# Three edits in one: where weight pieces are converted, turns moved from TensorE to VectorE, and tile addresses, in a sigmoid-attention and gated-MLP kernel

## Chip, cores and metric

One NeuronCore of a Trainium2 chip. The metric is the device time of one launch in microseconds (us), the median of three runs. TensorE (PE) multiplies; VectorE (DVE), ScalarE (ACT) and GpSimd (POOL) do the elementwise work; SyncE (SP) issues nearly all DMAs, in program order.

## The reference, cut to what matters

```python
# B, H, S, D = 4, 12, 448, 64;  d_model 768, d_ff 1024; w_in and w_out are float64
scores = q @ k.T / sqrt(D) - log(S);  attn = 1 / (1 + exp(-scores));  x = heads joined(attn @ v)
for layer in (1, 2):                  # first: relu; second: tanh-gelu, gain g_ln, residual
    h = act(x @ w_in);  u, v = h[..., :512], h[..., 512:]
    v_n = (v - mean) / sqrt(var + 1e-6) * g
    v_s = einsum('ts,bsd->btd', w_spatial, v_n) + b_spatial[None, :, None]
    x = (x if layer == 2 else 0) + (u * v_s) @ w_out
```

## The kernel before, in words

Every product is taken as three float32r products of a high and a low part (hi·hi, hi·lo, lo·hi): a value is cast to float32r (`hi`), and `lo` is the value less `hi`.

**Order.** Attention runs first, in twelve groups of four heads. Then come eight rounds, named here layer.batch: 1.0, 1.1, 1.2, 1.3, 2.0, 2.1, 2.2, 2.3. The order of instructions is written out by hand and each engine takes its own in that order. A round's TensorE steps are `hv` (the v half of w_in: four steps of 18 matmuls of 512 columns in an even round, three in an odd one, whose fourth key block went with the round before), `hu` (the u half, four steps of 18 matmuls of 448 columns), `sp` (the spatial product, four of 11) and `wo` (four of 18, in six PSUM banks). They run as hv1..hv3 (hv1, hv2 in an odd round), hu0, hu1, hu2, sp0, hu3, sp1, wo0, sp2, wo1, sp3, wo2, then the next round's hv0, then wo3. `hv`, `hu` and `sp` share two PSUM banks. After `sp(i)` VectorE makes `gt` and `u` from PSUM, ScalarE casts `gh`, and VectorE makes `gl`; `wo(i)` needs both. The next round's x is split (`split_x`) into `xh` and `xl` in three steps.

**Belts.** After nearly each TensorE step stands `fill()`, which moves side jobs on by one stage: first `spatial` (the spatial weights), then `belt` (weight pieces), then `chain` (the second half of the norm, and `gl`). A weight piece (`convert`, 128x256) is loaded as float64 words by DMA, rounded to float32 by four VectorE operations (L164, L168, L172, L177) and a ScalarE square (L163), and either split (ScalarE cast L185, VectorE subtract L187) or stored to DRAM (`kept`). `refetch` brings a kept piece back and splits it. Layer 1's w_in (24 pieces) is converted in attention, its w_out (12 pieces) and layer 2's w_in (24) in rounds 1.0 to 1.2; round 1.3, called the refill, refetches layer 2's w_in and converts its w_out (12).

**Turns.** Spatial weights are loaded in four blocks and turned by 16 TensorE transposes a layer into a PSUM bank (L218), then cast and subtracted (L219, L220). The output of a batch of layer 2 is turned in the rounds that follow by `store`: six transposes (L585) into PSUM, a ScalarE copy, and a DMA of rows of 3072 bytes; ten such stores in all. The last batch is turned at the end by `store_last`.

**Addresses.** A tile's byte address inside a partition is the sum of the sizes before it. In the kernel before, these begin 32 bytes behind a multiple of 64: x, bb, vh, vl, uh, ul, sh, sl, the normed v pairs (v0, v1), u, gt, gh, gl. These begin at a multiple of 64: ident, w, f, g, wsp, ops, xh, xl, oh, ol, vr.

Of the kernel before, what the change touches and what calls it, by code (L numbers as in the profile page):

```python
# [25 lines left out]
def tile_sigmoid_attention_two_gated_mlps(  # L26
# [120 lines left out]
    def convert(src, n, part, at, keep, early=False):  # L147
# [3 lines left out]
        w = stg.tile([P, PIECE, 2], I32, tag="w", name="w")  # L151
# [4 lines left out]
        g = stg.tile([P, PIECE], F32, tag="g", name="g", bufs=2)  # L156
# [18 lines left out]
        yield  # L175
# [26 lines left out]
    def load_w_sp(L, j, room, wait=1):  # L202

        w = stg.tile([CP, NCH, P], F32, tag="sp", name="wsp", bufs=2)
        src = L.w_sp.rearrange("(c p) s -> p c s", p=CP)
        if j < 3:
            nc.sync.dma_start(out=w, in_=src[:, :, j * P:(j + 1) * P])
        else:
            for r in range(0, P, REST):
                nc.sync.dma_start(out=w[:, :, r:r + REST], in_=src[:, :, 3 * P:])  # L210
        for _ in range(wait):
            yield
# [3 lines left out]
        t = room()  # L216
        for c in range(NCH):
            nc.tensor.transpose(t[:, c * CP:(c + 1) * CP], w[:, c, :], ident[:CP, :CP])  # L218
        nc.scalar.copy(out=L.sh[:, j, REST:], in_=t[:, :S])  # L219
        nc.vector.tensor_tensor(  # L220
            out=L.sl[:, j, REST:], in0=t[:, :S], in1=raw(L.sh[:, j, REST:]), op=ALU.subtract
        )
        yield
        for w in (L.sh, L.sl):
            nc.vector.tensor_copy(out=w[:, j, :REST], in_=raw(w[:, j, S:]))

    def load_w_sp_pair(L, j):
        yield from load_w_sp(L, j, bank, 7)
        yield
        yield from load_w_sp(L, j + 2, bank, 2)  # L230
# [24 lines left out]
    def load_vecs(L):  # L255
# [12 lines left out]
    kept = dram.tile([P, PIECE * l2.late], F32, name="kept")  # L268
    belt, chain, spatial = Belt(), Belt(), Belt()
    spatial.waiting = [load_w_sp(l1, j, lambda: two_banks()[:, 0]) for j in range(4)]  # L270


    def attention(apool, epool, ps_att, done):
# [52 lines left out]
        def low(n, eng):  # L326
            for j, t, e in zip((1, 3), turned[n], (nc.vector, eng)):
                e.tensor_tensor(
                    out=ops[n][:, j], in0=t, in1=raw(ops[n][:, j - 1]), op=ALU.subtract
                )  # L330
# [64 lines left out]
        load_qk(0)  # L395
        load_v(0)
        load_qk(1)
        turn(0)
        high(0)
        low(0, nc.vector)  # L400
        load_v(1)
        load_vecs(l1)
        for s in range(4 * NG + 2):
# [9 lines left out]
            if n + 1 < NG:  # L413
# [4 lines left out]
                elif r == 2:  # L418
                    low(n + 1, nc.gpsimd)
# [152 lines left out]
    def rows(pr, j):  # L572

        if j == 3:
            return [(slice(r * REST, (r + 1) * REST), out[2 * pr + r, 3 * P:]) for r in range(2)]
        return [(slice(0, P), out[2 * pr + j // 4, j % 4 * P:(j % 4 + 1) * P])]

    def store(pool, pr, j):
        x = xs[pr]
        o = pool.tile([P, DM], F32, tag="o", name="o", bufs=2)  # L580
        t = two_banks()
        half = DM // 2
        for m in range(KD):
            g, c = divmod(m * P, half)
            nc.tensor.transpose(t[:, g, c:c + P], x[:, m, j * P:(j + 1) * P], ident)  # L585
        nc.scalar.copy(out=o.rearrange("p (g f) -> p g f", g=2), in_=t[:, :, :half])
        for ps, dst in rows(pr, j):
            nc.sync.dma_start(out=dst, in_=o[ps])

    def store_last(o, pr, m):  # L590
# [11 lines left out]
        if m % 2:  # L602
# [5 lines left out]
            for ps, dst in rows(pr, 3):  # L608
                eng.dma_start(out=dst[:, ms], in_=o[ps, 0, ms])

    with tc.manual_schedule():
# [23 lines left out]
        with tc.tile_pool(name="fpool", bufs=1) as fpool:  # L635
# [3 lines left out]
            belt.waiting += [convert(*x, kept) for x in l2.pieces[:l2.late]]  # L639
# [111 lines left out]
```

## Time and profile before

| | |
|---|---|
| median of 3 runs | 627.3 us (626.49 to 628.46) |
| the profiled execution's own time | 629.11 us |
| its span, first to last instruction | 626.5 us |
| busy in the span: PE, DVE, ACT, POOL | 596.5, 385.9, 262.1, 95.7 us |
| mean granted TensorE clock | 0.985 |

Matmuls overlap, so PE counts as busy while only waiting for columns; the start-to-start distance of its instructions says more.

### The profile page before, as it was taken

The page shows a single profiled execution, that of the slowest core. Times are in us where ns is not written, and L with a number is a line of the kernel's source. Part 1 is how long each engine was busy: PE and PEld are TensorE (multiplying, and loading weights), DVE is VectorE, ACT ScalarE, POOL GpSimd, SP SyncE. Part 2 cuts the span into 40 slices and gives each one's busy share as a digit, 9 for nine tenths or more (in the row PEclk, how much of TensorE's full clock was granted, in tenths as well). Part 3 has the DMA queues.
Part 4 walks back from the last instruction along what each step waited for, and adds up shares of the span by engine and source line. Part 5 has one row for each costly group of instructions (what it writes and reads, how often), then busy time and mean ns, then how long its engine had stood idle before and what let it go on. Part 6 is the DMA issues. An engine that isn't in the chain of part 4 may idle for free.

```text
span 626.5 us, 9499 instructions
## 1 busy us (share of the span) xinstructions
PE 596.5 (95%) x3660; PEld 471.4 (75%) x3660; DVE 385.9 (62%) x770; ACT 262.1 (42%) x440; POOL 95.7 (15%) x121
## 2 busy tenths in 40 slices
PE   3999999999989899989999997899999999999996
PEld 2555555554779789978998996679889988998995
DVE  5399999996887867776452467772451543244123
ACT  3677777777344333424222453632113313221312
POOL 0164455453120010001000000010010001001000
PEclk9999999999999899989999998899999999999999
DMA  6646446541223224333200253300001000200103
GB/s 191 191 147 187 155 146 187 157 122 35 65 66 85 67 84 143 102 104 98 76 1 1 75 148 107 100 0 1 0 1 76 0 1 18 84 1 0 76 0 101
DMA packets 42044, 50.15 MB, mean 80 GB/s; under 512 B 9872, under 2 KB 30736, under 8 KB 42000
## 3 DMA queue, kind: packets, MB, share of 16 engines
q1 hardware_dynamic: 41840, 49.43, 25.9%
q8 instruction: 28, 0.46, 0.3%
q10 hardware_dynamic: 160, 0.13, 0.1%
q14 instruction: 16, 0.13, 0.1%
HBM read 40.90 MB, written 8.65 MB: 79 GB/s over the span
## 4 chain that ended last, share of the span: by engine, by line
PE 78%; DVE 13%; ACT 4%; DMA 2%; issue 2%; POOL 0%; SPq 0%; ACTq 0%; DVEq 0%; POOLq 0%
PE t L502 17%; PE t L456 13%; PE sc L342 12%; PE av L366 11%; PE sc L555 10%; PE t L521 9%; PE av L555 5%; DVE xl L445 2%; DVE f L168 2%; DVE f L172 1%; DVE f L177 1%; PE sc L585 1%; DVE f L164 1%; DVE st L466 1%; DMA w<-in_moe_w_out_dram 1%
## 5 line engine op out<-in xcount | busy, mean ns | idle before, releaser
L353 ACT ACTIVATE a<-sc,bias_s 128x896 f32<-128x896 f32 (+1 forms) x96 | 92.8, 1007 | 30.6 <-PE sc L342 30.3
L342 PEld LDWEIGHTS sc<-ops 32*128 32x128 f32 x1152 | 56.8, 191 | 46.5 <-ACT a L353 25.9
L342 PE MATMUL sc<-ops 32*128 32x448 f32 x1152 | 79.3, 394 | 10.0 <-ACT ops L324 8.0
L502 PE MATMUL t<-xh,uh 128*128 128x448 f32 x192 | 72.2, 376 | 4.0 <-ACT u L506 3.7
L456 PE MATMUL t<-vh,xh 128*128 128x512 f32 x168 | 68.5, 408 | 5.2 <-DVE sl L220 5.2
L502 PE MATMUL t<-xl,uh 128*128 128x448 f32 x192 | 71.2, 371 | 0.0
L502 PE MATMUL t<-xh,ul 128*128 128x448 f32 x192 | 71.2, 371 | 0.0
L468 POOL TENSOR_SCALAR rs<-mv 128x1 f32<-128x1 f32 x28 | 9.8, 351 | 389.1 <-DVE mv L467 389.1
L456 PE MATMUL t<-vh,xl 128*128 128x512 f32 x168 | 67.6, 402 | 0.0
L456 PE MATMUL t<-vl,xh 128*128 128x512 f32 x168 | 67.5, 402 | 0.0
L521 PE MATMUL t<-sh,v 128*128 128x448 f32 x224 | 65.8, 363 | 0.0
L534 ACT CAST gh<-u 128x448 fp32r<-128x448 f32 x32 | 18.1, 567 | 109.6 <-DVE u L533 109.6
L366 PE MATMUL av<-a,vt 128*64 128x448 f32 x288 | 62.7, 558 | 0.0
L466 DVE BATCH_NORM_STATS2 st<-vr 128x6 f32<-128x512 f32 x28 | 19.4, 694 | 63.6 <-ACT vr L462 63.6
L555 PE MATMUL sc<-gl,oh 128*128 128x448 f32 x128 | 48.8, 381 | 5.4 <-DVE gl L538 5.4
L177 DVE SCALAR_TENSOR_TENSOR f<-g,f 128x256 f32<-128x256 f32 x72 | 50.5, 701 | 1.9 <-ACT u L506 0.5
L529 DVE SCALAR_TENSOR_TENSOR gt<-t,gc,bb 128x448 f32<-128x448 f32 x16 | 10.9, 684 | 63.6 <-PE t L521 63.6
L555 PE MATMUL sc<-gh,oh 128*128 128x448 f32 x128 | 48.5, 379 | 0.0
L555 PE MATMUL sc<-gh,ol 128*128 128x448 f32 x128 | 48.2, 377 | 0.0
L521 PE MATMUL t<-sl,v 128*128 128x448 f32 x128 | 46.7, 365 | 0.0
L521 PEld LDWEIGHTS t<-sh,v 128*128 128x128 f32 x224 | 42.0, 187 | 3.4
L502 PEld LDWEIGHTS t<-xh,uh 128*128 128x128 f32 x192 | 36.5, 190 | 9.0 <-ACT u L506 4.5
(88 smaller groups left out, 1021.5 us busy)
## 6 DMA issues: line engine op xcount, KB each, us to landing
w<-in_moe_w_in_dram SPq DMA_DIRECT2D x48, 256.0 KB, 3.1
w<-in_moe_w_out_dram SPq DMA_DIRECT2D x24, 256.0 KB, 2.7
ink<-in_k_dram SPq DMA_DIRECT2D x12, 448.0 KB, 4.4
inq<-in_q_dram SPq DMA_DIRECT2D x12, 448.0 KB, 5.1
vt<-in_v_dram SPq DMA_DIRECT2D x48, 96.0 KB, 2.6
out_dram<-o SPq DMA_DIRECT2D x9, 384.0 KB, 2.6
kept<-f SPq DMA_DIRECT2D x24, 128.0 KB, 1.7
w<-kept SPq DMA_DIRECT2D x6, 256.0 KB, 3.2
```

The lines of the kernel that those rows point to most:

```text
L168: nc.vector.scalar_tensor_tensor(out=f.bitcast(U32), in0=low.bitcast(U32), scalar=29, in1=f.bitcast(U32), op0=ALU.logical_shift_right, op1 ...
L177: nc.vector.scalar_tensor_tensor(out=f, in0=g, scalar=TINY * TINY, in1=f, op0=ALU.is_ge, op1=ALU.mult)
L342: nc.tensor.matmul(sc[h // 2][:, h % 2, :S], w[ps, o:o + P], ops[n][ps, y, S * j:S * (j + 1)], start=(t == 0), stop=(t == 5), tile_positio ...
L353: nc.scalar.activation(a[:, 2 * x:2 * x + 2] if r < 3 else a[ps], sc[x][ps, :, :S], AF.Sigmoid, bias=bias_s[ps], scale=scale,)
L366: nc.tensor.matmul(avp[n][x][o * D:(o + 1) * D, :S], vt[:, h, r] if r < 3 else vr[ps, o], a[:, h] if r < 3 else a[ps, o], start=(r == 0), ...
L445: nc.vector.tensor_tensor(out=self.xl[:, c, :n], in0=src, in1=raw(self.xh[:, c, :n]), op=ALU.subtract)
L456: nc.tensor.matmul(ps[:, :FF], a, w[:, c, :], start=(c == 0 and n == 0), stop=(c == KD - 1 and n == 2),)
L466: nc.vector.bn_stats(out=st, in_=vr)
L502: nc.tensor.matmul(ps[:, :S], w, a, start=(c == 0 and n == 0), stop=(c == KD - 1 and n == 2))
L521: nc.tensor.matmul(ps[:, :S], a, w, start=(n == 0), stop=(n == len(todo) - 1))
L534: nc.scalar.copy(out=gh, in_=u)
L555: nc.tensor.matmul(self.o[m][:, :S], w, a, start=(i == 0 and n == 0), stop=(i == KF - 1 and n == 2),)
```

## The change

- `convert`: a piece that isn't early makes its four VectorE operations in one stage; `w` has four buffers and `g` three. All 36 pieces of layer 2 are converted in rounds 1.0 to 1.2 and kept; in the refill eight refetches (`w_o`) take the place of twelve conversions.
- `fill(new)`: hv steps start one piece, hu steps two, wo steps one (two in the refill); `sp` steps have no fill.
- `load_w_sp`: 32x32 blocks are placed by four DMAs of 448 runs of 128 bytes, one VectorE instruction turns all the blocks of `wsp` into `tsp`, ScalarE casts; no TensorE transpose, no PSUM.
- `store(pool, b, m)`: VectorE turns one 128x448 block of a finished batch into `y` (two buffers), and four DMAs write it as 448 runs of 128 bytes each. Six stores follow in each of the rounds 2.1, 2.2 and 2.3, two behind each of hu0, hu1, hu2.
- first group of attention: ScalarE casts k, VectorE's subtracts are ordered anew, and the loads of group 1 go ahead of v's.
- small tiles are padded or joined, so that every tile behind `ident` begins 32 bytes behind a multiple of 64.

```diff
     ident = const.tile([P, P], F32, name="ident")
-    bias_s = const.tile([P, 1], F32, name="bias_s")
-    load_s = const.tile([P, 1], F32, name="load_s")
-    mhalf = const.tile([P, 1], F32, name="mhalf")
+    small = const.tile([P, 40], F32, name="small")
+    bias_s, load_s, mhalf = [small[:, i:i + 1] for i in range(3)]
...
-        w = stg.tile([P, PIECE, 2], I32, tag="w", name="w")
+        w = stg.tile([P, PIECE, 2], I32, tag="w", name="w", bufs=4)
...
-        yield
+        if early:
+            yield
         f = f.bitcast(F32)
...
+    def load_w_sp(L, j):
+        w = stg.tile([P, S], F32, tag="sp", name="wsp", bufs=2)
+        src = L.w_sp.rearrange("(b t) s -> t b s", t=32)
+        for e in range(4):
+            at = j * P + 32 * e if j < 3 else 3 * P + 32 * (e % 2)
+            nc.sync.dma_start(
+                out=w[32 * e:32 * e + 32].rearrange("p (b s) -> p b s", s=32),
+                in_=src[:, :, at:at + 32],
+            )
+        yield
...
+        t = stg.tile([P, S], F32, tag="spt", name="tsp", bufs=2)
+        nc.vector.transpose(out=t, in_=w)
+        nc.scalar.copy(out=hi[:, REST:], in_=t)
+        nc.scalar.copy(out=hi[:, :REST], in_=t[:, 3 * P:])
         yield
+        nc.vector.tensor_tensor(out=lo[:, REST:], in0=t, in1=raw(hi[:, REST:]), op=ALU.subtract)
+        nc.vector.tensor_copy(out=lo[:, :REST], in_=raw(lo[:, S:]))
...
-            L.gc = wts.tile([P, KF], F32, tag="gc", name=f"gc{L.n}")
+            L.gc = wts.tile([P, 64], F32, tag="gc", name=f"gc{L.n}")[:, :KF]
...
-            nc.vector.tensor_copy(out=ops[n][:, 0], in_=tk)
+            if n > 0:
+                nc.vector.tensor_copy(out=ops[n][:, 0], in_=tk)
+            else:
+                nc.scalar.copy(out=ops[n][:, 0], in_=tk)
...
+            if n > 0:
+                part(nc.vector, 1, slice(0, S))
+                part(nc.gpsimd, 3, slice(0, S))
+            else:
+                part(nc.vector, 1, slice(0, P))
+                part(nc.vector, 3, slice(0, S))
+                part(nc.vector, 1, slice(P, S))
...
         load_qk(0)
+        load_qk(1)
         load_v(0)
-        load_qk(1)
...
-            st = pool.tile([P, 6], F32, tag="st", name="st", bufs=3)
-            mv = pool.tile([P, 2], F32, tag="mv", name="mv", bufs=3)
-            rs = pool.tile([P, 1], F32, tag="rs", name="rs", bufs=3)
+            st = pool.tile([P, 16], F32, tag="st", name="st", bufs=4)
+            st, mv, rs = st[:, :6], st[:, 6:8], st[:, 8:9]
...
+    def store(pool, b, m):
+        y = pool.tile([P, S], F32, tag="y", name="y", bufs=2)
+        x = xs[b // 2][:, m, (b % 2) * S:(b % 2 + 1) * S]
+        if b % 2 == 0:
+            nc.vector.transpose(out=y, in_=x)
+        else:
+            nc.vector.transpose(out=y[:, :3 * P], in_=x[:, REST:])
+            nc.vector.transpose(out=y[:, 3 * P:], in_=x[:, :REST])
+        dst = out[b].rearrange("(k t) d -> t k d", t=32)
+        for e in range(4):
+            ps, at = slice(32 * e, 32 * e + 32), m * P + 32 * e
+            nc.sync.dma_start(
+                out=dst[:, :, at:at + 32], in_=y[ps].rearrange("p (k d) -> p k d", d=32)
+            )
...
-            belt.waiting += [convert(*x, kept) for x in l2.pieces[:l2.late]]
+            belt.waiting += [convert(*x, kept) for x in l2.pieces]
...
-                if refill:
-                    belt.drain()
...
+                for j in range(1, 4 if b % 2 == 0 else 3):
+                    m.hv(b, j)
+                    fill(1)
+                if refill:
+                    fill(2, [refetch(lambda c=c: l2.part_v(c, slice(0, FF)), c * FF, FF, kept)
+                             for c in range(KD)])
                 for i in range(3):
                     m.hu(b, i)
-                    for x in pend[2 * i:2 * i + 2]:
-                        store(fpool, *x)
-                    fill(w_u(i))
+                    if m is m2 and b > 0:
+                        store(fpool, b - 1, 2 * i)
+                        store(fpool, b - 1, 2 * i + 1)
+                    fill(2, w_u(i))
                 m.sp(b, 0)
-                fill()
                 m.hu(b, 3)
-                fill(w_u(3) + [load_w_sp_pair(l2, j) for j in range(2)])
+                fill(2, w_u(3))
+                split_next(0)
                 m.sp(b, 1)
-                split_next(0)
-                fill()
                 m.wo(b, 0)
+                fill(1 + refill, w_o(0))
                 split_next(2)
-                fill(w_o(0))
                 m.sp(b, 2)
+                m.wo(b, 1)
+                fill(1 + refill, w_o(1))
                 split_next(4)
-                fill()
-                m.wo(b, 1)
-                fill(w_o(1))
                 m.sp(b, 3)
                 if refill:
                     load_vecs(l2)
-                fill()
+                    spatial.waiting = [load_w_sp(l2, j) for j in range(4)]
+                    spatial.tick(2)
                 m.wo(b, 2)
-                fill(w_o(2))
+                fill(1 + refill, w_o(2))
```

## Rows read from the trace of the kernel before

**Rows 1.** The page, part 1: busy time, share of the span, instructions.

```profile
PE 596.5 (95%) x3660; PEld 471.4 (75%) x3660; DVE 385.9 (62%) x770; ACT 262.1 (42%) x440; POOL 95.7 (15%) x121
```

**Rows 2.** The chain in order of time, rounds 2.0 and 2.1: start, us, what.

```profile
438.70 2.22 PE t L521 x11
440.92 2.47 PE sc L555 x12
...
450.57 4.21 PE t L456 x18
...
466.86 3.71 PE t L502 x18
470.56 1.31 PE sc L585 x12
```

**Rows 3.** Rounds 1.0 to 2.0: us, busy PE, PEld, DVE, ACT, POOL, clock, DMA, GB/s.

```profile
161.50:227.60 66.10, 60.73 (x279) 52.81 (x278) 52.39 (x134) 24.07 (x57) 6.40 (x13) 0.95 0.27 75
227.60:282.70 55.10, 52.97 (x244) 46.73 (x243) 39.37 (x96) 19.45 (x43) 3.65 (x6) 0.97 0.38 116
282.70:338.00 55.30, 55.30 (x261) 48.77 (x261) 26.54 (x56) 17.24 (x35) 4.44 (x8) 1.00 0.15 47
338.00:398.60 60.60, 55.12 (x259) 47.72 (x257) 39.01 (x87) 28.26 (x60) 2.81 (x6) 0.97 0.36 103
398.60:458.40 59.80, 58.03 (x261) 49.89 (x262) 29.77 (x67) 18.63 (x39) 3.73 (x8) 0.97 0.04 9
```

**Rows 4.** Who waited for whom: us in total, times, longest us.

```profile
PEld sc L555 <- DVE gl L538: 6.6, 4, 2.9
...
PE t L456 <- DVE sl L220: 5.2, 3, 2.4
...
PE t L502 <- ACT u L506: 3.7, 2, 2.9
```

**Rows 5.** VectorE in order of time, round 1.0: two pieces one behind the other.

```profile
187.41 0.29 DVE L164 TENSOR_SCALAR f<-w 128x256 int32<-128x256 int32 x1
...
189.21 0.28 DVE L164 TENSOR_SCALAR f<-w 128x256 int32<-128x256 int32 x1
```

**Rows 6.** Groups by line: busy us, mean ns of one, idle before.

```profile
L538 DVE TENSOR_TENSOR gl<-u,gh 128x448 fp32r<-128x448 f32 x32 | 19.9, 621 | 8.1 <-ACT gh L534 8.1
...
L316 DVE STREAM_TRANSPOSE tq<-inq 128x896 f32<-128x896 f32 x12 | 12.9, 1078 | 1.5 <-DMA inq<-in_q_dram 1.5
L311 DVE STREAM_TRANSPOSE tk<-ink 128x384 f32<-128x384 f32 x24 | 12.4, 552 | 9.1 <-DMA ink<-in_k_dram 9.1
...
L200 DVE TENSOR_TENSOR ul<-w,uh 128x384 fp32r<-128x384 f32 x8 | 4.3, 554 | 1.7 <-ACT uh L198 1.7
```

**Rows 7.** The first group of attention, VectorE and TensorE in order of time.

```profile
8.54 1.08 DVE L328 TENSOR_TENSOR ops<-tq,ops 128x896 fp32r<-128x896 f32 x1
...
9.68 2.23 PE L342 MATMUL sc<-ops 32*128 32x448 f32 x18 [0.54 <-DVE ops L328]
```

**Rows 8.** VectorE in round 2.1, the norm of its last hv step.

```profile
469.79 0.55 DVE L476 TENSOR_SCALAR vr<-vr,mv,rs 128x512 f32<-128x512 f32 x1 [0.77 <-POOL rs L471]
```

**Rows 9.** DMA issues by line: KB each, median us from issue to landing.

```profile
kept<-f SPq DMA_DIRECT2D x24, 128.0 KB, 1.7
...
wsp<-in_moe_w_sg_dram SPq DMA_DIRECT2D x2, 112.0 KB, 3.0
```

**Rows 10.** SP's issues in the refill, in order of time.

```profile
382.56 0.33 SPq L258 DMA_DIRECT2D bb<-in_moe_b_sg_dram  x1
...
390.89 0.92 SPq L210 DMA_DIRECT2D wsp<-in_moe_w_sg_dram  x2
```

**Rows 11.** The chain in the refill: a piece's load, issued next behind bb and gc.

```profile
383.95 5.22 DMA w<-in_moe_w_out_dram
```

**Rows 12.** Stretches in which wsp's two loads flow; columns as in rows 3.

```profile
392.80:393.20 0.40, 0.40 (x3) 0.37 (x2) 0.37 (x2) 0.38 (x2) 0.00 (x0) 1.00 0.97 217
393.20:394.20 1.00, 1.00 (x6) 0.92 (x5) 1.00 (x5) 1.00 (x1) 0.00 (x0) 1.00 0.44 100
```

More of the change, by code (lines that the diff above doesn't have):

```diff
@@ L200, in refetch @@
         nc.vector.tensor_tensor(out=lo, in0=w, in1=raw(hi), op=ALU.subtract)
[L202 to L212, printed above, removed]
+    def load_w_sp(L, j):
[8 more added lines that the diff above has]
+        yield
         if L.sh is None:
@@ L215, in load_w_sp @@
             L.sl = wts.tile([P, 4, SPAN], F32R, tag="sl", name=f"sl{L.n}")
[L216 to L222, printed above, removed]
-        yield
[L224 to L230, printed above, removed]
+        hi, lo = L.sh[:, j], L.sl[:, j]
+        t = stg.tile([P, S], F32, tag="spt", name="tsp", bufs=2)
+        nc.vector.transpose(out=t, in_=w)
+        nc.scalar.copy(out=hi[:, REST:], in_=t)
+        nc.scalar.copy(out=hi[:, :REST], in_=t[:, 3 * P:])
+        yield
+        nc.vector.tensor_tensor(out=lo[:, REST:], in0=t, in1=raw(hi[:, REST:]), op=ALU.subtract)
+        nc.vector.tensor_copy(out=lo[:, :REST], in_=raw(lo[:, S:]))
     class Belt:
@@ L267, in tile_sigmoid_attention_two_gated_mlps @@
     pieces(l2)
-    kept = dram.tile([P, PIECE * l2.late], F32, name="kept")
+    kept = dram.tile([P, PIECE * len(l2.pieces)], F32, name="kept")
     belt, chain, spatial = Belt(), Belt(), Belt()
-    spatial.waiting = [load_w_sp(l1, j, lambda: two_banks()[:, 0]) for j in range(4)]
+    spatial.waiting = [load_w_sp(l1, j) for j in range(4)]
     def attention(apool, epool, ps_att, done):
@@ L322, in high, with low, part @@
             tk, tq = turned[n]
-            nc.vector.tensor_copy(out=ops[n][:, 0], in_=tk)
+            if n > 0:
+                nc.vector.tensor_copy(out=ops[n][:, 0], in_=tk)
+            else:
+                nc.scalar.copy(out=ops[n][:, 0], in_=tk)
             nc.scalar.copy(out=ops[n][:, 2], in_=tq)
[L326 to L330, printed above, removed]
+        def low(n):
+            def part(eng, j, cols):
+                t, hi, lo = [
+                    t.rearrange("p (j f) -> p j f", j=2)[..., cols]
+                    for t in (turned[n][j // 2], ops[n][:, j - 1], ops[n][:, j])
+                ]
+                eng.tensor_tensor(out=lo, in0=t, in1=raw(hi), op=ALU.subtract)
+            if n > 0:
[5 more added lines that the diff above has]
+                part(nc.vector, 1, slice(P, S))
         def scores(n, r):
@@ L395, in attention @@
         load_qk(0)
+        load_qk(1)
         load_v(0)
-        load_qk(1)
         turn(0)
         high(0)
-        low(0, nc.vector)
+        low(0)
         load_v(1)
@@ L418, in attention @@
                 elif r == 2:
-                    low(n + 1, nc.gpsimd)
+                    low(n + 1)
             if n + 2 < NG:
@@ L607, in store_last @@
             )
-            for ps, dst in rows(pr, 3):
-                eng.dma_start(out=dst[:, ms], in_=o[ps, 0, ms])
+            eng.dma_start(out=out[2 * pr + 1, 3 * P:, ms], in_=o[REST:, 0, ms])
     with tc.manual_schedule():
@@ L644, in tile_sigmoid_attention_two_gated_mlps, with fill @@
                 nxt, nb = seq[n + 1] if n + 1 < len(seq) else (None, None)
-                last = m is m2 and b == B - 1
                 refill = m is m1 and b == B - 1
-                if refill:
-                    belt.drain()
-                def fill(more=()):
+                def fill(new, more=()):
                     if refill:
@@ L653, in fill @@
                     spatial.tick(1)
-                    belt.tick(1)
-                    if refill or m is m2 and b == 0:
-                        belt.tick(1)
+                    belt.tick(new)
                     chain.tick()
@@ L661, in split_next @@
                         nxt.split_x(nb, c, c + 2)
-                pend = []
-                if m is m2 and b > 0:
-                    pend = [((b - 1) // 2, j) for j in ((0, 1, 2) if b % 2 else (3, 4, 5, 6))]
-                for j in range(1, 4 if b % 2 == 0 else 3):
-                    m.hv(b, j)
-                    fill()
-                fill([refetch(lambda c=c: l2.part_v(c, slice(0, FF)), c * FF, FF, kept)
-                      for c in range(KD)])
                 def w_u(i):
```

30 lines of the change are left out of this document (8 added, 22 removed).

## The prediction

> **What bounds the kernel now.** I read the busy shares first, and they say that TensorE is the engine to look at and how far it can be off its own pace: 596.5 us of 626.5 are busy [rows 1], but a busy TensorE may be waiting inside. So the second view is the chain of waits in order of time, in rounds where nothing but TensorE stands in it [rows 2]. There 18 matmuls of hu take 3.71 us, 206.1 ns each; 18 of wo the same (12 in 2.47); 18 of hv with 512 columns 4.21, 233.9 ns each; 11 of sp 2.22, 201.8 ns each. A round without a wait is therefore 4 x 4.21 + 8 x 3.71 + 4 x 2.22 = 55.4 us when even and 51.2 with its three hv steps when odd.
>
> The third view holds the stretches against this [rows 3]. Round 1.2 takes 55.3: no loss. Round 1.0 takes 66.1 (10.7 lost), 1.1 55.1 (3.9), 1.3 60.6 (9.4), 2.0 59.8 (4.4). The lost time goes with a busy VectorE (52.4 us of 66.1 in 1.0, 26.5 of 55.3 in 1.2) and a clock under 1. The list of waits names it too: TensorE waits for gl, for the spatial weights' low part in the shared PSUM bank, and for ScalarE's u, which stands behind casts that wait for VectorE [rows 4]. So: attention and layer 2's later rounds are bound by TensorE; rounds 1.0, 1.1, 1.3 and 2.0 by VectorE's order. Half clock follows the waits: 1.0 has two long ones and a clock of 0.95, so 0.05 x 66.1 = 3.3 us are lost by the 1.2 GHz level, 1.65 behind each wait.
>
> **The change part by part**, against the profiled execution's own 629.1 us.
>
> *Start, -0.5.* The first scores' second product waits 0.54 us for VectorE's subtract of q, which stands behind that of k [rows 7]. In the new order only 128 columns a half of k stand before it, and these fit into ScalarE's cast of q. Bounds 0 and 0.54; group 1's loads ahead of v's are hidden, v being needed some 10 us later.
>
> *Output turns, -6.5.* Two stores of six transposes hold TensorE 1.31 us [rows 2], 0.655 each; ten go: 6.5. They run where nothing else binds, so all of it counts.
>
> *What takes their place.* VectorE turns 896 columns in 1078 ns and 384 in 552 [rows 6], 1.03 ns a column, so 448 in 0.62 us. Six a round are 3.7 us where VectorE is nearly idle: the work is hidden. Not hidden may be the buffers: the third turn needs the first y back, so it waits for four DMAs of 448 runs, and behind it in VectorE's queue stand sp0's gt and u. Zero is the end of the last hv step. The norm stands at +2.9 (469.79 against 466.86 [rows 2, 8]) and ends at +3.5; the first turn ends at +4.1. A DMA's latency is about 1.3 us (1.7 to landing for 128 packets [rows 9], less their flow). Call r the time that one DMA of 448 runs adds in a stream. The sixth turn waits for four stores, 16 DMAs: 4.2 + 1.3 + 16r; then it takes 0.6 and gt 0.7: 6.8 + 16r. TensorE asks for that bank at sp1: 4 x 3.63 + 2.22 = 16.7.
>
> r isn't in the trace, as no DMA writes runs of 128 bytes. Its nearest rows are two loads of 448 runs of 256 bytes: in one stretch they flow at 217 GB/s, 0.53 us for 448, in the next at 100, 1.15 us [rows 12]; SP needs 0.46 per issue (two in 0.92 [rows 10]). So r lies between 0.47 and 1.15. I take 0.7, nearer the quick end, since in the slow stretch the DMA engines were only 0.44 busy, so the packets were not the limit. SP issues these 24 DMAs in 11 us a round and has nothing else queued there. That gives 18.0 against 16.7: 1.3 us a round, +3.9 for three. Bounds: nothing at 0.47, 8.5 a round or 25.5 at 1.15.
>
> The Trainium skill, "DMA: Bandwidth & Descriptors", Specifications, speaks against this edit: under 512 bytes a transfer is not at line rate, because the DMA engine reads, modifies and writes. The trace agrees so far that small reads are dear (the stretch at 100 GB/s), and shows no small write. By that rule as a doubling of r to 1.4, the wait would be 12.5 us a round, 37.5 in all; it is a rival below.
>
> *Round 1.0, -2.8.* A piece costs VectorE 189.21 - 187.41 = 1.80 us with its split [rows 5], about 1.46 without. Twelve of the 16 pieces here are split. Layer 1's spatial turns leave TensorE (10.7 of loss hold about 1.6 us of them and their bank), but VectorE pays 0.62 for each turn. SP issues 16 DMAs for five, eight of them in attention where it is idle; the other eight, 3.7 us, go ahead of two or three pieces' loads, each used a TensorE step (3.7 us) later, so I count them hidden; if not, one piece is late by as much. Walked from the end of hv3: norm and one piece to +6.2, then one, two and two pieces with the low parts of v to +18.0, then gt 0.7; sp1 asks at 17.1: 1.6 late. gl0 stands behind two more pieces, at about 24, and wo0 asks at 21: 2.9. gl1 is some 1.3 late. So 5.8 us of waits and two falls of the clock, 2.1: 7.9 lost where 10.7 were. This is the softest term: from +2 to -6.
>
> *Rounds 1.1 and 1.2, -3.4.* Now 15 and 16 pieces, nearly all unsplit. Two in a hu fill are 2.9 us under 3.71 of matmuls, and none stands between gt and gl of one sp. So 1.1 loses 0.5 for 3.9. Round 1.2 gets 13 pieces more, 19 us on top of 26.5 of 55.3: still free. If not, it is a rival.
>
> *Refill 1.3, -1.4.* Twelve conversions (1.80) become eight refetches (0.55 each [rows 6]) and TensorE's turns go, so the waits for sl L220 go. But the spatial loads are now issued behind bb and gc, which wait for sp3's gt, and their turns stand on VectorE ahead of gl3. Zero is the end of sp3: bb issues at +0.7. The load next behind bb and gc landed 383.95 + 5.22 - 382.56 = 6.6 us after bb's issue [rows 10, 11]; the first of the eight spatial DMAs takes its place: +7.3, the eighth 7r later, +12.2. Turn 0.62, two subtracts 1.1, gl3 0.62 [rows 6]: +14.5. wo3 asks for gl3 at 3.71 + 4.21 + 0.2 = 8.1. The wait is 6.4 us (4.8 to 9.6 by r), with the clock 8.0, where 9.4 were lost.
>
> *Round 2.0, -3.4.* Its 4.4 came from the conversions left over; two refetches and the last spatial blocks remain, 1.0 allowed.
>
> *Addresses, -6.7.* Of the four matmul steps, sp alone has both operands 32 bytes behind a multiple of 64 (v and sh); hu has xh, hv xh, wo oh at a multiple. And sp alone is 4.3 ns quicker per 448 columns [rows 2]. After the change all are placed as in sp. If that is the cause, hu and wo in the seven rounds other than 1.0 gain 1008 x 4.3 = 4.3 us, and hv 432 x 5.5 = 2.4 (233.9 against 213.3 + 15.1, sp's surplus). Round 1.0 is VectorE's, so its share is not counted. Lower bound 0.
>
> The Trainium skill, "TensorE: Matmul & The Clock Gate", in "Wait — 56ns, not 53.3ns?", gives a warm start-to-start of columns over 2.4 GHz and some 2.5 ns, whatever the address: 189 ns for 448 columns. The trace differs, at 202 and 206; by that rule addresses would give nothing, which is a rival below.
>
> *End, -0.3.* `store_last` issues one DMA fewer behind each pair, 0.46 of issue, partly hidden.
>
> **Sum.** -0.5 - 6.5 + 3.9 - 2.8 - 3.4 - 1.4 - 3.4 - 6.7 - 0.3 = -21.1: 629.1 becomes 608.0. The median of the runs lies 1.8 below the profiled time, so 606.2.
>
> **Rivals.**
> 1. *VectorE is held by y* (the side of slower). Small writes flow slower than small reads. For: rows 12's slow stretch, 24 DMAs a round. Against: the quick stretch, and rounds of over 50 us with the queue else empty. Without its 3.9 the change gains 25.0; it turns slower from 8.9 us a round on, r = (16.7 + 8.9 - 6.8) / 16 = 1.18, just beyond the slow bound. At 1.4: 602.3 + 37.5 = 640. Chance 0.12.
> 2. *The addresses do nothing*; sp's spacing has another cause, such as its stationary tiles. For: nothing in the trace shows an address at work. Against: three steps of different tiles share 206 to 207, one differs. 612.9. Chance 0.22.
> 3. *The pieces weigh more than walked*: 1.1 gains nothing, and 1.2 loses what 1.0 loses today less its turns, 8.8. 606.2 + 3.4 + 8.8 = 618. For: 1.0's 52.4 us of VectorE with 16 pieces. Against: 12 of those were split and four spatial blocks lay among them. Chance 0.11.
> 4. *The refill's wait stays away*, the spatial loads landing sooner: 8 us less, 598. Against: the load behind gc took 5.22. Chance 0.07.
>
> **How the numbers follow.** My case has 0.48 and is 600 to 612 by its own bounds. The range 596 to 620 takes in rivals 2 to 4 and stops before the first. Under 0.3% (1.9 us) is about what this kernel's three runs can't tell from no change. All but rival 1 are faster: 0.87 with a little taken off; rival 1 gives 0.10 slower and 0.03 same.
>
> **What would show each step.** No L585 or L218 in the groups. hu, wo and hv at about 202, 202 and 228 ns: else rival 2. In rounds 2.1 to 2.3, VectorE's turns released by DMAs of y, and sp1 late by 1 us: by 9 or more it is rival 1. Stretches: 1.0 about 63, 1.1 about 51, 1.2 about 54, 1.3 about 58, 2.0 about 55. In 1.3 a wait of wo3 for gl of some 6 us, with the turn before it released by wsp's DMA. I am most likely wrong in r, in 1.0's walk and in the cause of sp's 4.3 ns.

## The result and the profile after

The changed kernel takes 609.46 us in the median of four runs (608.56 to 611.24) against 627.88 for the kernel before on the same chip: a ratio of 0.9714, 95% interval 0.9683 to 0.9744. It is 18.4 us faster where 21.1 were forecast; 609.5 lies inside the range of 596 to 620 and 3.3 us above the forecast of 606.2. The profiled execution is the slowest of the four, 611.24 us with a span of 609.4; that of before had 626.5, so the two traces differ by 17.1 us.

The page of the profile after, busy time and share of each engine, which answers to [rows 1]:

```profile
PE 581.1 (95%) x3568; PEld 462.5 (76%) x3568; DVE 402.5 (66%) x790; ACT 255.7 (42%) x435; POOL 96.3 (16%) x121
```

VectorE has 16.6 us more to do than before and the kernel is quicker: what counts is where the work stands. The stretches of the rounds, from one hv1 to the next (1.0, 1.1, 1.2, 1.3, 2.0, 2.1, 2.2, and 2.3 with the end), against [rows 3]; columns are the stretch, its length, busy time of each engine (instructions), granted clock, DMA share, GB/s:

```profile
160.90:228.05 67.15, 60.23 (x263) 52.80 (x262) 53.82 (x131) 24.77 (x60) 7.41 (x13) 0.92 0.26 68
228.05:280.25 52.20, 50.93 (x244) 45.30 (x243) 38.77 (x92) 18.47 (x41) 2.68 (x6) 1.00 0.38 114
280.25:338.85 58.60, 56.63 (x262) 49.89 (x261) 42.40 (x100) 20.43 (x45) 3.60 (x8) 0.97 0.36 108
338.85:394.20 55.35, 52.16 (x244) 46.68 (x243) 31.10 (x62) 24.15 (x48) 3.33 (x6) 0.97 0.40 105
394.20:449.65 55.45, 55.26 (x262) 48.72 (x261) 27.27 (x53) 19.78 (x42) 4.71 (x8) 1.00 0.07 22
449.65:500.05 50.40, 50.40 (x244) 45.49 (x243) 24.16 (x43) 11.17 (x21) 2.67 (x6) 1.00 0.18 28
500.05:554.45 54.40, 54.40 (x262) 48.77 (x261) 26.89 (x54) 12.68 (x24) 3.81 (x8) 1.00 0.16 26
554.45:609.40 54.95, 49.62 (x250) 44.39 (x248) 22.94 (x40) 10.08 (x18) 1.91 (x4) 0.98 0.24 51
```

Rounds 2.1 and 2.2 run without any wait, so 50.4 us odd and 54.4 even is the new pace; before it was 51.2 and 55.4. Against before, 1.0 lost 1.05 us, 1.1 won 2.9, 1.2 lost 3.3, 1.3 won 5.25 and 2.0 4.35. The same stretches of before for 2.1, 2.2 and 2.3 are 53.0, 58.0 and 57.1 us: 2.6, 3.6 and 2.2 won. The rest, some 0.6, is attention. TensorE's waits from 150 to 450 us (us in total, times, longest), against [rows 4] and this line of before, whose row in [rows 4] is that of the weight loads (PEld):

```profile
PE sc L555 <- DVE gl L538: 5.4, 3, 2.5
```

The changed kernel:

```profile
PE sc L564 <- DVE gl L547: 8.4, 4, 3.2
PE t L511 <- ACT vr L472: 2.9, 1, 2.9
PE t L511 <- ACT u L515: 2.1, 2, 1.9
```

The waits for the spatial weights in PSUM are gone; those for gl stay, 8.4 us where 5.4 were (matmuls with matmuls): 2.1, 1.2 and 2.0 at wo0 of 1.0, 1.1 and 1.2, and 3.2 at wo3 of 1.3. The chain of waits in 2.1, against [rows 2] (start, us, what):

```profile
458.08 10.94 PE t L511 x54
469.03 2.23 PE t L530 x11
471.26 3.65 PE t L511 x18
...
477.13 2.43 PE sc L564 x12
...
492.54 4.08 PE t L466 x18
```

hu takes 202.6 ns a matmul (206.1 before), wo 202.5 (206), hv 226.7 (233.9), but sp 202.7 (201.8). In round 1.2, behind the wait for gl, first the clock falls (granted 0.51 from 314 to 317 us, the 1.2 GHz level); then all but hv run slower at the full clock:

```profile
313.38 0.63 DVE gl L547
...
319.34 2.27 PE t L530 x11
321.62 2.48 PE sc L564 x12
```

These are 206.4 and 206.7 ns a matmul, sp too, and they last until the next hv step.

### The profile page after: what moved, and what is told of

The parts are those of the page before. It is cut to its first block, busy times and chain, and to the rows that moved or that the text cites. A ratio compares the mean times of both kernels' runs of the same rounds, so it can differ in the third digit from the quotient of the medians.

```text
span 609.4 us, 9527 instructions
## 1 busy us (share of the span) xinstructions
PE 581.1 (95%) x3568; PEld 462.5 (76%) x3568; DVE 402.5 (66%) x790; ACT 255.7 (42%) x435; POOL 96.3 (16%) x121
## 4 chain that ended last, share of the span: by engine, by line
PE 77%; DVE 12%; ACT 5%; issue 3%; DMA 1%; SPq 1%; POOL 0%; DVEq 0%; ACTq 0%; POOLq 0%
PE t L511 13%; PE sc L352 12%; PE t L466 12%; PE sc L564 12%; PE av L376 11%; PE t L530 10%; PE av L564 6%; DVE f L169 1%; DVE f L173 1%; DVE st L475 1%; DVE f L179 1%; DVE xl L455 1%; SPq L211 1%; DVE f L165 1%; ACT vr L472 1%
## 5 line engine op out<-in xcount | busy, mean ns | idle before, releaser
L363 ACT ACTIVATE a<-sc,small 128x896 f32<-128x896 f32 (+1 forms) x96 | 92.8, 1006 | 30.6 <-PE sc L352 30.3
L477 POOL TENSOR_SCALAR st<-st 128x1 f32<-128x1 f32 x28 | 9.3, 332 | 372.5 <-DVE st L476 372.5
L466 PE MATMUL t<-vh,xh 128*128 128x512 f32 x168 | 65.5, 390 | 0.0
L466 PE MATMUL t<-vl,xh 128*128 128x512 f32 x168 | 65.5, 390 | 0.0
L466 PE MATMUL t<-vh,xl 128*128 128x512 f32 x168 | 65.4, 389 | 0.0
L493 ACT CAST v<-vr 128x512 fp32r<-128x512 f32 x24 | 14.9, 621 | 62.6 <-DVE vr L485 62.6
```

Source lines behind the costliest of these rows:

```text
L363: nc.scalar.activation(a[:, 2 * x:2 * x + 2] if r < 3 else a[ps], sc[x][ps, :, :S], AF.Sigmoid, bias=bias_s[ps], scale=scale,)
L466: nc.tensor.matmul(ps[:, :FF], a, w[:, c, :], start=(c == 0 and n == 0), stop=(c == KD - 1 and n == 2),)
L477: nc.gpsimd.tensor_scalar(out=rs, in0=mv[:, 1:2], scalar1=EPS, scalar2=None, op0=ALU.add)
L493: nc.scalar.copy(out=pair[0], in_=vr)
```

## The experiments

Each kernel was timed in five rounds against the kernel before; ratios are to that, on their own chip. The times of this table are medians.

| kernel | us | ratio, interval |
|---|---|---|
| changed | 609.5 | 0.971 (0.968 to 0.974) |
| address edit taken back | 613.8 | 0.977 (0.974 to 0.980) |
| all tiles at a multiple of 64 | 609.5 | 0.970 (0.967 to 0.974) |
| output turned by TensorE | 617.7 | 0.983 (0.980 to 0.986) |
| one buffer for y | 643.3 | 1.025 (1.022 to 1.028) |
| low parts first | 607.4 | 0.966 (0.963 to 0.970) |
| + low parts on GpSimd | 610.3 | 0.973 (0.971 to 0.975) |
| + cast a tick behind the turn | 607.9 | 0.969 (0.966 to 0.971) |
| + spatial weights early | 600.6 | 0.957 (0.955 to 0.960) |
| ++ half the work of 12 pieces left out | 597.4 | 0.952 (0.948 to 0.955) |
| ++ kept pieces moved, paddings | 604.0 | 0.962 (0.959 to 0.964) |
| ++ paddings alone, sp too | 598.8 | 0.954 (0.951 to 0.956) |
| changed, paddings of 64 | 608.1 | 0.969 (0.967 to 0.972) |

A "+" stands on "low parts first", a "++" on "spatial weights early". No kernel took back the new order of the pieces or VectorE's spatial turns alone: what these two are worth is read from the stretches and not shown by a run.

**Addresses.** First the edit was taken back:

```diff
-            L.gc = wts.tile([P, 64], F32, tag="gc", name=f"gc{L.n}")[:, :KF]
+            L.gc = wts.tile([P, KF], F32, tag="gc", name=f"gc{L.n}")
...
-            st = pool.tile([P, 16], F32, tag="st", name="st", bufs=4)
-            st, mv, rs = st[:, :6], st[:, 6:8], st[:, 8:9]
+            st = pool.tile([P, 6], F32, tag="st", name="st", bufs=3)
+            mv = pool.tile([P, 2], F32, tag="mv", name="mv", bufs=3)
+            rs = pool.tile([P, 1], F32, tag="rs", name="rs", bufs=3)
```

> The changed kernel with only the address edit taken back: gc is 16 bytes again and the small statistics three tiles of their own, so xh, xl, oh, ol lie at a multiple of 64 and vh, uh, sh, gh, v 32 behind one, as before the change. Theory (the place of a tile sets the matmul's pace): hu and wo return from 202.6 to 206 ns and hv from 227.5 to 233.9, sp stays at 202; 1008 x 4 ns + 432 x 6 ns and the share of round 1.0 give about +7, 616 to 617 us against 609.5. Rival (the paces changed for another reason, such as the order of the work): hu, wo, hv stay at 202 to 203 and 227 to 228 ns and the time stays at 608 to 611.

It took 613.8 us, 4.3 more than the changed kernel. Its chain of waits in 2.2:

```profile
513.87 11.14 PE t L512 x54
525.01 2.22 PE t L531 x11
...
533.17 2.47 PE sc L565 x12
...
548.75 4.21 PE t L466 x18
```

The steps are back at 206.3, 201.8, 205.8 and 233.9 ns, so the places of the tiles do set the pace. The edit is worth 4.3 us and not 7, because the changed kernel's steps don't stay at 202. The second question was what it is about the places:

```diff
-    small = const.tile([P, 40], F32, name="small")
+    small = const.tile([P, 48], F32, name="small")
```

> The changed kernel with the first small tile 192 bytes long in place of 160: every operand of hv, hu, sp and wo begins at a multiple of 64, so both sides of each matmul still agree, only at the other remainder. Theory A (both operands must have the same remainder): nothing changes, 202 to 203 ns and 609 us. Theory B (the 32 behind 64 itself is what is quick): sp, hu and wo all go to 206 ns and hv to 234; with sp's 352 matmuls in it about +8, 617 us.

609.5 us, and the paces are those of the changed kernel (means of hv, hu, sp and wo 227.3, 202.7, 203.1, 203.6): theory A. It isn't the 32 bytes behind 64 that count, as the prediction had it, but where the two operands lie to each other.

As the order of the work is the same too, its rounds 1.0 and 1.2 can be set beside those of the changed kernel:

```profile
160.90:228.10 67.20, 58.92 (x263) 51.39 (x262) 53.85 (x131) 24.86 (x60) 7.43 (x13) 0.95 0.24 68
280.30:337.55 57.25, 55.29 (x261) 48.51 (x260) 42.34 (x100) 20.45 (x45) 3.60 (x8) 1.00 0.35 111
```

1.2 has the same wait of 2.0 us for gl, but the granted clock did not fall behind it (1.00 for 0.97), and the round takes 57.25 us for 58.60. 1.0 is as long at a clock of 0.95 as at 0.92: TensorE does not set its length.

Then the operands were set apart:

```diff
-                L.vl = wts.tile([P, KD, FF], F32R, tag="vl", name=f"vl{L.n}")
+                L.vl = wts.tile([P, KD * FF + 16], F32R, tag="vl", name=f"vl{L.n}")
+                L.vl = L.vl[:, :KD * FF].rearrange("p (c f) -> p c f", c=KD)
... the same for ul3; and st with bufs=5
```

> The changed kernel with paddings of 64 bytes: the two operands of hv stay at one remainder of 128, those of hu, sp and wo are 64 apart. Theory (the difference of the two places modulo 128 sets the pace: 0 gives 202.5 or, in some stretches, 206.6 ns for 448 columns, 64 gives 201.5 always, 32 and 96 give 206.5; for 512 columns 0 is the quickest, 227.4): hu, sp and wo all at 201.5 to 202 with no stretch at 206, 1360 x 1.8 ns or 2.4 us less, 607 us. Rival (only the remainder of 64 counts, and stretches at 206 come from the waits ahead of them): as changed, 202.5 with stretches at 206, 609.5.

608.1 us, some 1.4 less than the changed kernel, at overlapping intervals. The paces say more than the time. In 2.2:

```profile
509.94 10.81 PE t L514 x54
520.74 2.23 PE t L533 x11
...
528.79 2.40 PE sc L567 x12
...
544.03 4.17 PE t L469 x18
```

hu and wo run at 200 ns, quicker than at any place before, and no stretch of them is at 206. But hv went back to 231.7, though its operands have the same remainder modulo 128: modulo 256 they are 128 apart. The mean ns from one matmul's start to the next inside a step, rounds behind 1.0, stand here behind the distance of the two operands in bytes (moving minus stationary, modulo 256; the addresses are added up from the sizes of the tiles, not read from a trace):

| kernel | hv | hu | sp | wo |
|---|---|---|---|---|
| before | -32: 233.5 | 32: 206.6 | -64: 201.8 | 32: 206.4 |
| address edit taken back | -32: 233.4 | 32: 206.3 | -64: 201.8 | 32: 206.4 |
| changed | 0: 227.3 | 0: 202.9 | 0: 203.8 | 0: 204.2 |
| all at 64 | 0: 227.3 | 0: 202.7 | 0: 203.1 | 0: 203.6 |
| output turned by TensorE | -64: 233.3 | 64: 201.3 | -64: 202.3 | 0: 205.9 |
| paddings of 64 | 128: 232.2 | 64: 200.2 | -64: 202.5 | 64: 200.9 |
| kept pieces moved, paddings | 0: 227.3 | -64: 202.4 | -64: 202.4 | 64: 200.7 |

That made a rule that could be tried out: hv at 0, the rest at +64. The paddings stand on "spatial weights early":

```diff
+                L.vl = wts.tile([P, KD * FF + 48], F32R, tag="vl", name=f"vl{L.n}")
... ul3 with 48 more; gc 96 wide in place of 64; st with bufs=5
```

> The kernel with low parts first and spatial weights early (600.6 us), and paddings so that the moving operand of hv begins at the same remainder of 256 as the stationary one, and those of hu, sp and wo 64 behind theirs (moving minus stationary +64). Theory (the mean pace goes with that difference modulo 256, as the kernels so far show it: +64 gave 200.2 to 201.4 ns for 448 columns, -64 201.8 to 202.5, 0 202.5 to 204.0, 32 or -32 206.1 to 206.7; for 512 columns 0 gave 227.3 and all else 232 to 233.4): hu, sp and wo at 200 to 201 ns in the mean, hv at 227.3; 1360 x 2.4 ns, -3.3, 597.3 us. Rival (those means are other things, such as which step follows a wait, or sp does not follow the rule): 599.5 to 601.5 us.

598.8 us. The means of hv, hu, sp and wo are 227.6, 200.3, 200.1 and 200.9, sp at 200 for the first time; the chain in 2.2:

```profile
500.65 10.80 PE t L516 x54
511.45 2.20 PE t L535 x11
...
519.47 2.40 PE sc L569 x12
...
534.70 4.13 PE t L471 x18
```

So the rule held for the paces. The time fell by 1.8 us, not by the 3.3 expected (the two intervals overlap): a round without a wait is 0.4 us shorter (50.0 and 54.05), seven such rounds would be 2.8, and short waits for ScalarE and VectorE give a part back, such as 0.4 in 1.1.

**The output's turns.** `store` was put back on TensorE, as in the kernel before:

```diff
-    def store(pool, b, m):
-        y = pool.tile([P, S], F32, tag="y", name="y", bufs=2)
+    def store(pool, pr, j):
+        o = pool.tile([P, DM], F32, tag="o", name="o", bufs=2)
+        t = two_banks()
... (the rest as before the change; gc 16 wide in place of 64)
```

> The changed kernel with the output of three batches turned by TensorE again, through PSUM and ScalarE, as before the change; all else as changed (gc 64 bytes in place of 256 to make room). Theory (VectorE's turns and their 128-byte stores are wholly hidden, r is small): ten stores of 0.655 us come back, +6.5, 616 us. Rival (the stores of y still hold something up, as the 3.9 us that I forecast): only +2.6, 612 us.

617.7 us, 8.2 more than the changed kernel. Pairs of stores stand in the chain again, and beside them another pace, since the smaller gc moved the tiles:

```profile
448.93 7.93 PE t L466 x34
456.86 3.62 PE t L511 x18
460.48 1.31 PE sc L594 x12
461.79 3.61 PE t L511 x18
```

Ten stores at 0.655 us are 6.55. By the table, the other places cost hv 6.0 ns x 432 and wo 1.7 x 504, and give back hu 1.6 x 504 and sp 1.5 x 308: +2.2 us. Together 8.7, close to the 8.2 measured. So the turns are worth 6.5, and nothing of it is lost to y.

How near that is to a loss the next kernel shows:

```diff
-        y = pool.tile([P, S], F32, tag="y", name="y", bufs=2)
+        y = pool.tile([P, S], F32, tag="y", name="y", bufs=1)
```

> The changed kernel with one buffer for y in place of two, so that each of the six turns of a round waits until the four stores of the one before it have left. By the prediction's own way of counting, with r = 0.54 us as the 56 KB stores flow at 105 GB/s: a turn then costs 0.62 + 1.3 + 4 x 0.54 = 4.1 us, the sixth ends at 24.6 us and gt of sp 0 at 25.3, against the 16.7 at which sp 1 asks: 8.6 us a round, 26 for three, 635 us. With r = 0.7: 4.7 a turn, 12 us a round, 645. Rival (the stores are released sooner, or TensorE's asking is not what VectorE's queue decides): less than 2 us a round, 609 to 615.

643.3 us. The waits of TensorE and of VectorE behind 440 us:

```profile
PE t L530 <- DVE gt L538: 27.0, 3, 9.2
```

```profile
DVE y L586 <- DMA out_dram<-y: 34.6, 10, 3.7
DVE y L588 <- DMA out_dram<-y: 16.3, 5, 3.6
```

Fifteen turns wait 3.4 us each, where 1.3 + 4 x 0.54 = 3.5 was the reckoning, and sp1 is late by 9 us a round, where 8.6 was. Only the clock was left out of the sum: behind each wait TensorE is at 1.2 GHz for a while, so that 2.1, at a mean granted clock of 0.92, took

```profile
447.80:509.85 62.05, 52.91 (x244) 47.28 (x243) 24.37 (x43) 11.07 (x21) 2.67 (x6) 0.92 0.14 23
```

11.65 us more than the 50.40 of the changed kernel for 9.2 of wait.

**The waits for gl.** In the changed kernel's 1.2, VectorE's queue reads (start, us):

```profile
309.36 0.63 DVE L542 TENSOR_TENSOR u<-gt,u 128x448 f32<-128x448 f32 x1
309.91 0.29 DVE L165 TENSOR_SCALAR f<-w 128x256 int32<-128x256 int32 x1
...
313.04 0.42 DVE L179 SCALAR_TENSOR_TENSOR f<-g,f 128x256 f32<-128x256 f32 x1
313.38 0.62 DVE L547 TENSOR_TENSOR gl<-u,gh 128x448 fp32r<-128x448 f32 x1
```

Two pieces stand between u and gl, and wo0 waits for gl. So the order was turned round: from hu0 on, the low parts (`chain`) go ahead of the spatial turns and the pieces:

```diff
+                    if first:
+                        chain.tick()
                     spatial.tick(1)
                     belt.tick(new)
-                    chain.tick()
+                    if not first:
+                        chain.tick()
... first = False ahead of the hv steps, True behind them
```

> The changed kernel with the ticks in another order: in every fill from hu 0 on the low parts (norm's and gl) are put on VectorE's queue ahead of the spatial turns and the pieces of conversion; after the hv steps as changed. Theory (what is lost in 1.0, 1.2 and 1.3 is gl standing behind pieces or behind a turn that waits for its load, and the half clock behind each such wait): wo 0 waits 2.3 in 1.0, 2.1 in 1.2 and wo 3 3.3 in 1.3, with about 1.6 us of clock each; these 7.7 to 12.5 us go, 597 to 602 us. Rival (VectorE has more work than these stretches hold, so that the order only moves the wait): 1.0, 1.2 and 1.3 keep their 67, 58 and 55 us, 607 to 611 us.

607.4 us, 2.1 less: the rival's time, but not its stretches. The waits for gl went (0.6 us of 8.4 are left, and 1.3 for gh); 1.1, 1.2 and 1.3 fell to 50.4, 55.65 and 50.4 us. But 1.0 stayed at 67.0, and 2.0 rose from 55.45 to 61.65 with a new wait of its second hv:

```profile
PE t L466 <- ACT vr L472: 4.5, 1, 4.5
```

The spatial weights of layer 2 are turned behind gl3 now, and it is ScalarE that stands: 8.7 us at casts that wait for such turns, with hv's activation behind them in its queue. Therefore those weights were loaded, and two blocks turned, ahead of the last sp of 1.3:

```diff
                 def fill(new, more=(), turns=()):
+                    for j in turns:           # in the refill only
+                        next(sp2[j], None)
...
-                fill(2, w_u(3))
+                fill(2, w_u(3), (0, 1))                       # hu3: two loads
-                fill(1 + refill, w_o(1))
+                fill(1 + refill, w_o(1), (0, 1, 2, 3))        # wo1: two turns, two loads
-                    spatial.waiting = [load_w_sp(l2, j) for j in range(4)]
-                    spatial.tick(2)
... casts and subtracts behind sp3: two blocks in the fill of wo2, two in those of hv0 and wo3
```

> The same kernel (low parts first), and besides layer 2's spatial weights are loaded during round 1.3 (two blocks behind hu 3, the others behind wo 1) and two of the turns made there; casts and low parts stay behind the last sp of 1.3, which still reads layer 1's. Theory (what the refill still costs, 4.7 us at the second hv of 2.0 with low parts first and 3.3 at wo 3 without, is the spatial loads issued late and VectorE standing at the turn for them): rounds 1.3 and 2.0 fall from 112.0 to some 105, the pace without a wait (50.4 + 54.4), 600 us. Rival (ScalarE's casts and VectorE's subtracts of refetched weights are what fills that stretch): 112 stays, 606 to 608.

600.6 us, as the theory had it. Its 1.3 and 2.0 take 50.35 and 54.80 us at a clock of 1.00:

```profile
333.75:384.10 50.35, 50.35 (x244) 45.43 (x243) 32.22 (x64) 24.55 (x50) 2.59 (x6) 1.00 0.45 116
384.10:438.90 54.80, 54.71 (x262) 48.74 (x261) 27.05 (x52) 19.60 (x42) 4.43 (x8) 1.00 0.07 22
```

**Round 1.0.** Its 67 us are 12.6 above the pace without a wait. Three kernels asked what holds it.

```diff
-        nc.vector.tensor_tensor(out=lo[:, REST:], in0=t, in1=raw(hi[:, REST:]), op=ALU.subtract)
+        eng = nc.gpsimd if L.n == 1 else nc.vector
+        eng.tensor_tensor(out=lo[:, REST:], in0=t, in1=raw(hi[:, REST:]), op=ALU.subtract)
... and GpSimd for the subtract L189 of every piece
```

> The kernel of the run before (low parts first in the fills), and besides the low parts of layer 1's spatial weights and of the 12 pieces of w_out converted in round 1.0 are subtracted by GpSimd, not VectorE: 12 x 0.42 and 4 x 0.82 us, 8.3 off VectorE's 53.8 in that stretch. Theory (round 1.0 is bound by the amount of VectorE's work; the order only moves the wait, as 1.0 stayed at 66 to 67 us with low parts first): the stretch falls by about 6, 601 us. Rival (the bound is the ring of ScalarE and VectorE, each standing at the head of its queue for the other): waits of hu for vr (3.1) and u (2.1) stay and the time is 606 to 608.

610.3 us, 2.9 more than low parts first alone: outside both. Though 16 subtracts and four copies left VectorE, its busy time in 1.0 did not fall (55.0 us, 54.3 without). One of VectorE's four operations on a piece, first without, then with GpSimd's subtracts:

```profile
L173 DVE SCALAR_TENSOR_TENSOR f<-w,f 128x256 int32<-128x256 int32 x16 | 6.8, 425 | 0.5
```

```profile
L173 DVE SCALAR_TENSOR_TENSOR f<-w,f 128x256 int32<-128x256 int32 x15 | 8.5, 564 | 0.5
```

425 became 564 ns in the mean. Eleven of the 15 still took 424 to 427 ns; the four that ran beside a subtract of GpSimd's took 839 to 1253, such as this one beside the subtract below it:

```profile
193.16 0.84 DVE L173 SCALAR_TENSOR_TENSOR f<-w,f 128x256 int32<-128x256 int32 x1
```

```profile
192.98 0.74 POOL L189 TENSOR_TENSOR ol<-f,oh 128x256 fp32r<-128x256 f32 x1 [1.78 <-ACT oh L187]
```

So this kernel took no work away from VectorE, and tells nothing about amount.

```diff
         nc.vector.transpose(out=t, in_=w)
+        if L.n == 1:
+            yield
         nc.scalar.copy(out=hi[:, REST:], in_=t)
... tsp with three buffers
```

> The same kernel (low parts first), and besides, for layer 1's spatial weights alone, the casts are put one tick behind VectorE's turn, so that ScalarE no longer stands at a cast whose turn is still in VectorE's queue, with the activation of hv behind it (three turned buffers in place of two). Theory of amount: VectorE's work is the same, so 1.0 stays within 1 us and the time is 606 to 608. Rival (the ring): ScalarE's 7.0 us before those casts go, and with them the wait of hu for vr (3.1 us) and half clock behind it (1.5): 602 to 603.

607.9 us, no change. ScalarE no longer stands at those casts, and the two waits of hu only trade places: 1.6 for vr and 3.9 for u, where 2.9 and 1.9 were.

```diff
+        if early or keep is not None:
             nc.vector.scalar_tensor_tensor(out=f.bitcast(U32), in0=low.bitcast(U32), scalar=29, ...
             nc.vector.scalar_tensor_tensor(out=f, in0=high, scalar=-0x40000000, ...
```

> The kernel with low parts first and spatial weights early (600.6 us), and the 12 pieces of layer 1's w_out, all converted in round 1.0, leave out two of the four VectorE instructions that put a float together, so the output isn't the reference's: 24 x 0.425 = 10.2 us off VectorE's 54 in that stretch, without any work for GpSimd. Theory (1.0 is bound by the amount of VectorE's work ahead of each step): its loss of 12 us, waits of hu 3.1 and 2.1 among them, falls by 6 to 9, 592 to 595 us. Rival (the ring of ScalarE and VectorE at the hv steps, where only 3 of these 12 stand): the two waits of hu stay above 4 us together, 597 to 600 us.

Its median is 597.4 us (runs from 595.1 to 599.7), 3.2 below the kernel it stands on. That is in the rival's range, and so are hu's two waits, 4.2 us together. Yet in the trace, of an execution of 595.3 us, 1.0 takes 61.75 us in place of 66.80, with 10.3 us less of VectorE's work:

```profile
PE t L514 <- ACT vr L475: 2.3, 1, 2.3
PE t L514 <- ACT u L518: 1.9, 1, 1.9
PE av L567 <- DVE ol L190: 0.7, 1, 0.7
```

Of the waits hu's two are left, and 0.7 for ol; those for gt, gh and gl in the second half, 2.8 us, went. So the second half of 1.0 is held mostly by the amount of VectorE's work. The first half isn't, or not by these pieces alone: ScalarE and VectorE stand there in turn for one another around the norm, and which link must be cut wasn't found.

A last try moved the four kept pieces out of 1.0 and set paddings:

```diff
+                    if n == 0 and len(belt.waiting) <= len(l2.pieces):
+                        new = 0
...
-                    fill(1)
+                    fill(1 + (n == 1))
... vl 16 and ul3 48 wider, st with bufs=5
```

> The kernel with low parts first and spatial weights early (600.6 us), with paddings such that the operands of hv share one remainder of 256 and those of hu, sp and wo are 64 apart, and with the four kept pieces that stood in the last steps of 1.0 moved into the hv steps of 1.1 and 1.3. Theory on places: hv 227.4 and the others 200.5 to 202 ns with no stretch at 206.6, 1360 x 2 ns, -2.7. Theory on pieces: the waits of wo in the second half of 1.0 (0.55, 0.46, 1.1, 0.46, 0.85) go, -2 to -3; 1.1 stays at 50.4. Together 595 to 596 us. Rival: hv needs another distance than 0 (in the padded kernel before, at 128, it took 232 ns), and VectorE is late in 1.0 for the split pieces alone, so that nothing is won: 600 us.

604.0 us, 3.4 worse than without. 1.0 did not change (66.70 us). Of the waits of its second half only the 1.1 for gt went, as it did with paddings alone; so it is the split pieces that weigh there and not the kept ones; and two pieces a step in the hv steps of 1.1 made sp wait 2.2 us for gt, so that 1.1 took 54.5 us for 50.45. Its hu, at -64, ran at 202.4 and not at 200.

## Why the prediction held, point by point

The direction and the reading were right: TensorE bounds attention and layer 2's later rounds, VectorE's order the others, and the gain came from turns, pieces and places. The size is in part luck. Between the two traces 17.1 us were won where the sum has 21.1. With the share of the places taken out of each round, rounds 1.0 (3.9), 1.2 (3.8), 1.1 (1.3) and the places (2.4) were taken too hopefully, by some 11 us, and y (3.9), the refill (3.0) and 2.0 (0.5) too gloomily, by some 7: two errors that offset each other.

- *Start, -0.5.* Right: the second product of the first scores doesn't wait any more, and all that lies ahead of 1.0 is 0.6 shorter.
- *Output turns, -6.5.* Right, by the stores put back.
- *y, +3.9.* Nothing. VectorE's turns do wait for the stores, 19.7 us in three rounds, but no wait of TensorE follows. The mechanism was right to a fraction: sixth turn at 4.2 + 1.3 + 16r + 0.6. The trace has r: 24 DMAs are issued between 462.2 and 474.4 us, 0.53 each, of which SP's issue takes 0.49, and the sixth turn ends 14.8 us behind the last hv; the formula gives 14.6. Mis-sized was r, 0.7 in place of 0.53, near its lower bound: SP's issue nearly fills it. Runs of 128 bytes flowed out at about 105 GB/s and landed 1.9 us after issue. The Trainium skill, "DMA: Bandwidth & Descriptors", Specifications, has a read-modify-write under 512 bytes. The doubling of r that the prediction took from it doesn't show, and the slow stretch that it read as agreeing had DMA engines only 0.44 busy. Rival 1 fell with it; the kernel with one y shows that it was one buffer away.
- *Round 1.0, -2.8.* Wrong: +1.05, though inside the bounds given. The walk followed VectorE alone from the end of hv3 and put the first wait at sp1. The first waits came earlier, at hu1 and hu2, for ScalarE's vr and u, which are late because ScalarE stands at casts that wait for VectorE. gl0 was late by 2.1 us, where the walk had 2.9. The waits are 6.9 us together, near the 5.8 walked; the clock took more, 0.08 x 67.15 = 5.4 us where two falls were put at 2.1, though the same text has 1.65 behind each. The clock alone doesn't explain the loss either: all at 64 has a clock of 0.95 and the same length.
- *Round 1.1, -3.4.* -2.9, and 0.8 of it is the places: gl0 stayed late by 1.2.
- *Round 1.2, 0.* Wrong: +3.3. That "none stands between gt and gl of one sp" was the step that failed: hu3's fill is issued behind sp0 and its two pieces are made between u and gl. The wait is 2.0 us; half clock behind it and the pace of 206.6 ns are the rest. Without the fall of the clock, as in all at 64, the round loses 1.9. A part of rival 3, whose 8.8 was too much.
- *Refill, -1.4.* -5.25, some 0.8 of it from the places. Right cause, too long: wo3 waited 3.2 us, not 6.4, and the turn ahead of gl3 stood 6.3 us for the load of wsp. The second four of the eight loads came 1.3 us behind the first, not 4r = 2.8. That the loads were issued late behind gt was the cause is shown by the kernel that issues them early. Rival 4 fell.
- *Round 2.0, -3.4.* -4.35 with its share of the places.
- *Addresses, -6.7.* 4.3. The effect is real, so rival 2 fell; the condition was another (the distance of the two operands, not 32 behind 64). By the table hv gained the 2.4 us forecast and a little more, but hu and wo only 2.8 of 4.3: stretches at 206.6 were left, and the changed places took sp from 201.8 to 203.8. Nor did three steps share 206 to 207 before, as rival 2 has it: hu and wo did, and hv, of 512 columns, took 233.9. The rule in the Trainium skill, "TensorE: Matmul & The Clock Gate", "Wait — 56ns, not 53.3ns?", has no place for an address. Rows of this kernel differ by 3% with it.

## What to carry to other kernels

Ask of a queue what stands between a value and its last consumer: moving low parts ahead of optional work took four waits away and won 2.1 us; the next 6.7 came only when what stood next in line, the loads that a cast waits for, was moved forward too. A wait of TensorE costs its length and what follows it: the 2.0 us in 1.2 cost 4.2 against the pace of 54.4 where the clock fell behind it, and 2.9 where it did not. For a dense row of matmuls compare the start-to-start distance of steps that should be alike: here 2 to 6 ns a matmul hung on paddings of under 600 bytes in all.

## What the hardware showed that was not expected

- The pace of 128x448 float32r matmuls goes with the distance of the two operands' addresses modulo 256: 200.1 to 201.3 ns at +64, 201.8 to 202.5 at -64, some 202.6 or 206.6 at 0, 206.3 to 206.6 at 32. For 512 columns 227.3 to 227.6 at 0 and 232.2 to 233.5 at the other distances (-32, -64 and 128). Whether the modulus is 256 or a larger one, no run tells apart.
- At 0 there are two paces. A stretch at 206.6 begins mostly behind a wait and lasts until the next hv step or wait, and where the output is turned by TensorE wo has a mean of 205.9. What chooses between them stays open.
- A subtract on GpSimd of 128x256 takes 0.84 us to VectorE's 0.42, and an operation of VectorE's on 128x256 that ran beside it took 839 to 1253 ns in place of 425.
- One ScalarE table load of 1.28 us stands at the change from relu to gelu, inside the refill's chain.
